# Scatters through disjoint views, later gathers, and copies kept in order in a routed expert layer

## The chip, the cores and the metric

The kernel runs on one core of a Trainium2 chip. The metric is the device time of one execution in microseconds (us); the median of three runs of the kernel before is 864.54 us (863.58 to 864.58). The profiled execution, from which all durations below are read, took 866.19 us, of which 864.5 us are its span from the first instruction to the last.

## The reference

Three layers on 3072 tokens of 512 numbers each, all float32:

```
attention: 4 batches x 8 heads x 768 positions x 64; a key is kept when it is one of the
           8 first or one of the 96 last; a bias by distance; softmax; a @ v
dense:     h = x @ w_in (512 x 2048); g = h if h > 0 else exp(h) - 1; y = g @ w_out
routed:    chosen = (y @ w_skip) > 0; expert = argmax(y @ w_gate) over 8; gate = its softmax weight
           out = y, and for chosen tokens  out = y + gate * (relu(y @ w1[expert]) @ w2[expert])
           (w1[e] 512 x 1024, w2[e] 1024 x 512)
```

## The kernel before

Every float32 product is made of three float16 products of high and low halves, so TensorE (PE) has much to do: 6233 matmuls. The tokens go through attention and the dense layer in 8 blocks (m = 0 to 7) of 3 tiles of 128 tokens; the attention of the next block is woven into the dense steps of the current one. A dense step (m, f), with f = 0 to 15, makes the product h (L439), a chain on ScalarE (ACT) and VectorE (DVE, L446) and GpSimd (POOL, L450) that ends in gs, and two steps later the product y from it (L460).

**Routing.** When a block's y is done, `route` copies it to yt (L504), writes it to the output (L506, or L589 for the last block), turns it with DMA transposes, takes the gate logits, and `place` computes for each token a slot in `xg`, a DRAM buffer of 8 experts x 256 rows of 514 numbers. `scatter(t)` (L582) is an indirect DMA on POOL's queue that writes the 128 rows of tile t into `xg`; a token that is not chosen gets a slot out of bounds and isn't written. Each row carries in its last column the token's number.

**Experts.** `ex_gather` (L635, SyncE's queue, SP) reads 128 rows of an expert back from `xg` to yg; `ex_tokens` (L644, L645) splits them into float16 halves eyh (one buffer for it) and turns them by DMA transpose (L646) to eyT. `ex_first` (L660, then L662 on ACT and L664 on DVE) and, two steps later, `ex_second` (L676) are the two products; the last step of an expert's tile adds the result to the row (eres, L684), copies the row's token number to integer (ix, L686) and scatters to the output (L687, POOL). `ex_prep` splits one piece of expert weights per tile and step (L623 on ACT, L624 on DVE) from er, loaded on SP (L608, L610) two pieces ahead into two stage buffers; a pair of loads waits for the split of the pair before.

`ex_tail` writes the order of this: steps s_ = 0 to 23 are experts 0 to 2 with their first tile of 128 slots, 24 to 47 the same experts with their second tile, then experts 3 to 6 with both tiles at once, then expert 7. The first tiles' gathers and splits stand earlier, in the dense steps f = 11 and f = 13 of the last block (L896). The last block itself is routed inside `ex_tail` (`ROUTE_LAST`: place at s_ = 11, its three scatters and its output writes at s_ = 12), the second tiles are gathered at s_ = 15, split at s_ = 22, 24 and 26, and the gathers of expert 3 stand at s_ = 38 and 39.

**What sets the order.** Each engine takes its instructions in a fixed order. A scheduler makes that order ahead of the run: it takes the instructions by the order in the program, but an instruction whose inputs are ready by its own reckoning passes others that are not. So an instruction can come ahead of its place in the program. `pin` (L72) ties an instruction behind the one written just before it on its engine. L623 and L644 are pinned, L686 is not. Waits between instructions come from a tracker of accesses to tiles and DRAM buffers: two indirect writes to `xg` may hit the same rows for all it knows, so the second waits until the first has landed, and a gather waits for all scatters before it.

Of the kernel before, what the change touches and what calls it, by code (L numbers as in the profile page):

```python
# [1 line left out]

# [10 lines left out]
U32 = DT.uint32  # L13
# [8 lines left out]
NT, DM, FF = 3072, 512, 2048  # L22
# [3 lines left out]
TB = 3  # L26
# [36 lines left out]
class Fast:  # L63
# [400 lines left out]
    def route_init(self):  # L464
        nc = self.nc
        self.wg = self.ct([P, ND, E + 1], F32, "wg")
        nc.sync.dma_start(self.wg[:, :, 0:E], self.a["moe2_w_gate"].rearrange("(c p) e -> p c e", p=P))
        nc.sync.dma_start(self.wg[:, :, E:E + 1], self.a["moe2_w_skip"].rearrange("(c p o) -> p c o", p=P, o=1))

        self.wgs = self.ct([P, ND, 2, E + 1], F16, "wgs")  # L470
        t = self.ct([P, ND, E + 1], F32, "wgt")
        nc.vector.tensor_scalar(t, self.wg, GS, None, ALU.mult)
        nc.vector.tensor_copy(self.wgs[:, :, 0, :], t)
        nc.vector.tensor_tensor(self.wgs[:, :, 1, :], t, self.wgs[:, :, 0, :], ALU.subtract)
        nc.vector.tensor_tensor(t, t, t, ALU.mult)
        self.wgm = self.ct([P, 2], F32, "wgm")
        nc.vector.tensor_reduce(out=self.wgm[:, 0:1], in_=t[:, :, 0:E], op=ALU.max, axis=AX.XY)
        nc.vector.tensor_reduce(out=self.wgm[:, 1:2], in_=t[:, :, E], op=ALU.max, axis=AX.X)
        self.esum = self.ct([P, TB], F32, "esum")
        nc.vector.memset(self.esum, 0.0)  # L480
        self.xg = self.dp.tile([E * CAP, ROW], F32, name="xg")
        z = self.zrow = self.mp.tile([P, ROW], F32, tag="yt", name="zrow", bufs=4)
        nc.gpsimd.memset(z[:, 0:DM + 1], 0.0)
        nc.gpsimd.memset(z[:, DM + 1:ROW], OOB)
# [5 lines left out]
    def route(self, m):  # L490

        nc, mp = self.nc, self.mp
        sm = mp.tile([P, 7, TB], F32, tag="sm", name=f"sm_{m}", bufs=2)
        oh = mp.tile([P, TB, E], F16, tag="oh", name=f"oh_{m}", bufs=2)
        pos = mp.tile([P, TB], I32, tag="pos", name=f"pos_{m}", bufs=2)
# [84 lines left out]

        def scatter(t):
            nc.gpsimd.indirect_dma_start(  # L582
                out=self.xg[:, :], out_offset=bass.IndirectOffsetOnAxis(ap=pos.bitcast(U32)[:, t:t + 1], axis=0),
                in_=yts[t][:, :], in_offset=None, bounds_check=E * CAP - 1, oob_is_err=False)

        def write():
# [4 lines left out]
        if last:  # L591
            return [evac, lambda: [turn(t) for t in range(TB)],
                    lambda: gate(0), lambda: gate(1), lambda: gate(2), place,
                    lambda: [scatter(t) for t in range(TB)], write]
        ops = dict(e=evac, a=lambda: turn(0), b=lambda: turn(1), c=lambda: turn(2), A=lambda: gate(0), B=lambda: gate(1),
                   C=lambda: gate(2), p=place, x=lambda: scatter(0), y=lambda: scatter(1), z=lambda: scatter(2))
        return [lambda w=w: [ops[o]() for o in w] for w in ROUTE]

# [69 lines left out]
    def ex_second(self, e, f, tiles):  # L668
        nc = self.nc
        hs = self.ehs.pop((e, f, tiles[0]))  # L670
        for j, t in enumerate(tiles):
            if f == 0:
                tag, bufs = ("pv", 1) if (e % 2 and t if e >= NX else e + t == 0) else ("acc", 3)
                self.eo[(e, t)] = self.ps.tile([P, DM], F32, tag=tag, name=f"eo_{e}_{t}", bufs=bufs)
            for n, (s_, x) in enumerate(((0, 0), (0, 1), (1, 0))):
                nc.tensor.matmul(self.eo[(e, t)], hs[:, s_, j * P:(j + 1) * P],  # L676
                                 self.ew[(e, 4 + f // 2, f % 2)][:, x, :],
                                 start=(f == 0 and n == 0), stop=(f == F2 // P - 1 and n == 2))
        if f < F2 // P - 1:
            return  # L680
        for t in tiles:
            y = self.eyg.pop((e, t))
            r = self.mp.tile([P, DM], F32, tag="yT", name=f"eres_{e}_{t}", bufs=2)
            nc.vector.scalar_tensor_tensor(r, self.eo.pop((e, t)), y[:, DM:DM + 1], y[:, 0:DM], ALU.mult, ALU.add)  # L684
            ix = self.xp.tile([P, 1], I32, tag="ix", name=f"ix_{e}_{t}", bufs=2 * E)
            nc.vector.tensor_copy(ix, y[:, DM + 1:DM + 2])  # L686
            nc.gpsimd.indirect_dma_start(  # L687
                out=self.out[:, :], out_offset=bass.IndirectOffsetOnAxis(ap=ix.bitcast(U32)[:, 0:1], axis=0),
                in_=r[:, :], in_offset=None, bounds_check=NT - 1, oob_is_err=False)

    def ex_tail(self, prep, rest):
        both = tuple(range(CAP // P))
        steps = [(e, f, (t,)) for t in both for e in range(NX) for f in range(F2 // P)]
        n0 = len(steps)
        steps += [(e, f, both) for e in range(NX, E - 1) for f in range(F2 // P)]
        steps += [(E - 1, f, (t,)) for t in both for f in range(F2 // P)]
        flag = self.flag()
        nf = F2 // P
        pieces = dict(zip("etABCpsw", self.route(NM - 1)))
        for s_, (e, f, tiles) in enumerate(steps):  # L700
            for x in ROUTE_LAST.get(s_, ""):
                pieces[x]()
            if s_ == 0:
                self.htags = "s0", "s1", "h"
            if s_ == 3:
                self.htags = ("h",)
            if s_ == 13:
                self.htags = "h", "s0", "h", "s1"
            if s_ == 15:
                for x in range(NX):  # L710
                    self.ex_gather(x, 1)
            for x in range(NX):
                if s_ == 22 + 2 * x:
                    self.ex_tokens(x, 1)
            if s_ == n0 - 10:
                self.ex_gather(NX, 0)
            if s_ == n0 - 9:
                self.ex_gather(NX, 1)
            if s_ in (n0 - 5, n0 - 3):
                self.ex_tokens(NX, (s_ - n0 + 5) // 2)  # L720
            if len(tiles) == 2 and e + 1 < E:
                if f == 1:
                    for t in both:
                        self.ex_gather(e + 1, t)
                if f in (3, 5):
                    self.ex_tokens(e + 1, (f - 3) // 2)
            self.ex_first(e, f, tiles)
            if s_ and rest:

                self.moe_y(*rest.pop(0))  # L730
            for _ in tiles:
                prep()
            if s_ >= 40:
                next(flag, None)
            if s_ == len(steps) - 1:
                for _ in flag:
                    pass
                self.flag_sum()
            if s_ >= XLAG:
                self.ex_second(*steps[s_ - XLAG])  # L740
        for x in steps[-XLAG:]:
            self.ex_second(*x)
        self.flag_all()
# [444 lines left out]
```

## Time and profile before

| | |
|---|---|
| median of the runs (lowest, highest) | 864.54 us (863.58, 864.58) |
| profiled execution: its own time, its span | 866.19 us, 864.5 us |
| PE busy | 817.8 us, 95% |
| DVE, ACT, POOL busy | 571.4, 530.0, 174.5 us |
| chain that ended last | PE 72%, DVE 11%, DMA 10% |
| mean granted TensorE clock | 0.977 |

A row of a timeline gives start, length, engine, line, operation, output <- inputs and how many instructions were merged; in brackets how long the engine had been idle before, and what ended that. PE shows as busy when it runs slowly too, so the granted clock belongs beside it. A DMA's row on SP or POOL is its issue alone; its landing is seen in the chain of waits or in the wait of whoever needs it.

### The profile page before, as it was taken

To read this page: it belongs to the slowest core of one execution; us is meant where nothing else is said; L and a number is where in the kernel's file an instruction comes from. 1 tells how busy PE (TensorE), PEld (TensorE's weight loads), DVE (VectorE), ACT (ScalarE), POOL (GpSimd) and SP (SyncE) were. 2 spreads that over 40 slices of the span, in tenths; PEclk is the share of its full clock that TensorE was granted. 3 is DMA by queue.
4 is the path that set the end of the run, shared out by engine and by line. 5 is a ranking of instruction groups with operands and counts; after the bars stand their busy time and mean duration, and the time that the engine had idled before them with its cause. 6 is when DMAs were issued, how large, how long until landed. Compare 5 with 4: busy or idle time off the path is not lost.

```text
span 864.5 us, 17637 instructions
## 1 busy us (share of the span) xinstructions
PE 817.8 (95%) x6233; PEld 479.4 (55%) x6233; DVE 571.4 (66%) x1951; ACT 530.0 (61%) x1310; POOL 174.5 (20%) x201
## 2 busy tenths in 40 slices
PE   6997989999999999999999999999998869999995
PEld 4773445555555555555555555555555637666663
DVE  6997997575467567556666765644666846878622
ACT  4775767777767677767776776645655425555311
POOL 1001112123222322321322232232231010101110
PEclk9997999999999999999999999999999988999998
DMA  7999973644686487688659656321646779779510
GB/s 293 256 298 253 245 217 91 132 111 102 201 205 162 137 214 142 175 191 189 152 139 229 154 124 146 77 51 43 189 154 159 228 225 211 247 242 275 157 44 26
DMA packets 185394, 148.80 MB, mean 172 GB/s; under 512 B 152208, under 2 KB 154256, under 8 KB 181200
## 3 DMA queue, kind: packets, MB, share of 16 engines
q1 hardware_dynamic: 182096, 141.59, 63.0%
q0 software_dynamic: 3200, 5.99, 1.9%
q8 instruction: 51, 0.84, 0.4%
q14 instruction: 47, 0.39, 0.2%
HBM read 94.82 MB, written 21.08 MB: 134 GB/s over the span
## 4 chain that ended last, share of the span: by engine, by line
PE 72%; DVE 11%; DMA 10%; issue 4%; POOL 1%; ACT 1%; SPq 0%; POOLq 0%; DVEq 0%; ACTq 0%
PE h L439 25%; PE y L460 24%; PE eh L660 7%; PE eo L676 6%; PE s L239 5%; PE pv L324 4%; DMA eyT<-eyh 3%; DMA xg<-yt,pos 2%; DMA yg<-xg 2%; DVE ew L624 2%; DVE wt L408 2%; DVE wt L409 1%; PE warm L354 1%; DMA xT<-xs 1%; DVE w L416 1%
## 5 line engine op out<-in xcount | busy, mean ns | idle before, releaser
L439 PE MATMUL h<-xT,w 128*128 128x384 f16 x1536 | 274.9, 329 | 4.1 <-DMA xT<-xs 4.1
L460 PE MATMUL y<-w,gs 128*128 128x512 f16 x1152 | 271.4, 381 | 0.0
L439 PEld LDWEIGHTS <-w 128*128 128x128 f16 x1536 | 146.8, 99 | 106.4 <-issue 9.7
L450 POOL TENSOR_TENSOR gs<-e,gs 128x384 f16<-128x384 f32 x128 | 126.1, 987 | 393.9 <-ACT gs L449 329.2
L460 PEld LDWEIGHTS <-gs 128*128 128x128 f16 x1152 | 110.8, 98 | 119.9 <-issue 2.7
L446 DVE SCALAR_TENSOR_TENSOR e<-e,h 128x384 f32<-128x384 f32 x128 | 70.4, 551 | 99.6 <-ACT e L444 94.1
L449 ACT ACTIVATE gs<-e 128x384 f16<-128x384 f32 x128 | 66.7, 522 | 86.1 <-DVE e L446 84.9
L253 ACT ACTIVATE p<-p,st 128x232 f32<-128x232 f32 (+1 forms) x192 | 89.2, 465 | 38.4 <-DVE st L248 37.7
L660 PE MATMUL eh<-eyT,ew 128*128 128x128 f16 (+1 forms) x1152 | 103.6, 243 | 7.6 <-DMA eyT<-eyh 5.6
L676 PE MATMUL eo<-ew,ehs 128*128 128x512 f16 x384 | 102.0, 388 | 8.1 <-DVE ehs L664 8.1
L660 PEld LDWEIGHTS <-ew 128*128 128x128 f16 x1152 | 88.7, 101 | 32.8 <-issue 6.7
L624 DVE SCALAR_TENSOR_TENSOR ew<-er,ew 128x512 f16<-128x512 f32 x128 | 90.5, 725 | 15.9 <-ACT ew L623 14.5
L443 ACT ACTIVATE e<-h 128x384 f32<-128x384 f32 x128 | 61.6, 481 | 58.5 <-PE h L439 54.5
L662 ACT ACTIVATE ehs<-eh 128x128 f16<-128x128 f32 (+1 forms) x96 | 29.9, 311 | 102.3 <-PE eh L660 99.8
L248 DVE CUSTOM_DVE_ANT_0 p<-s,tab 128x232 f32<-128x232 f32 (+1 forms) x192 | 67.1, 377 | 20.3 <-PE s L239 18.6
L623 ACT ACTIVATE ew<-er 128x512 f16<-128x512 f32 x128 | 75.4, 620 | 4.5 <-DMA er<-in_moe_w 4.2
L283 DVE TENSOR_TENSOR ph<-p,ph 128x464 f16<-128x464 f32 x68 | 43.1, 648 | 40.2 <-ACT ph L282 40.2
L444 ACT ACTIVATE e<-e 128x384 f32<-128x384 f32 x128 | 66.6, 520 | 2.5
L664 DVE SCALAR_TENSOR_TENSOR ehs<-eh,ehs 128x128 f16<-128x128 f32 (+1 forms) x96 | 31.9, 332 | 36.9 <-ACT ehs L662 36.7
L676 PEld LDWEIGHTS <-ehs 128*128 128x128 f16 x384 | 35.4, 99 | 36.7 <-DVE ehs L664 12.7
L687 POOL DMA_INDIRECT out<-eres,ix x16 | 16.9, 1053 | 161.9 <-DVE eres L684 117.7
L239 PE MATMUL s<-qh 64*128 64x232 f16 (+1 forms) x432 | 40.0, 254 | 3.1 <-DVE st L248 2.5
(171 smaller groups left out, 849.4 us busy)
## 6 DMA issues: line engine op xcount, KB each, us to landing
er<-in_moe_w SPq DMA_DIRECT2D x64, 512.0 KB
wr<-in_wf SPq DMA_DIRECT2D x16, 1024.0 KB
wc<-in_wf SPq DMA_DIRECT2D x16, 1024.0 KB
qk<-in_qk SPq DMA_DIRECT2D x20, 720.0 KB
out<-yt SPq DMA_DIRECT2D x24, 256.0 KB
rawv<-in_vp SPq DMA_DIRECT2D x21, 256.0 KB
xg<-zrow SPq DMA_DIRECT2D x16, 257.0 KB
yg<-xg SPq DMA_DIRECT2D x16, 257.0 KB
```

What stands on the lines that cost most here:

```text
L239: nc.tensor.matmul(sp[j], q[r, hp, KW:], k[r, hp, KW - w:KW], start=(x == 0), stop=(x == len(mm) - 1))
L248: nc.vector.tensor_tensor_reduce(pw[:, j, :], sp[j], self.tab[:, h, :] if i else self.tab0[:, h, :], -0.125, 3e38, ALU.add, ALU.min, st[:, ...
L253: nc.scalar.activation(pw[:, j, :], pw[:, j, :], AF.Exp, bias=st[:, 0, h:h + 1], scale=-1.0, accum_out=st[:, 1, h:h + 1])
L439: nc.tensor.matmul(hps, wi[:, s_, c, :], xT[:, x * ND + c, :], start=(n == 0), stop=(n == 3 * ND - 1))
L446: nc.vector.scalar_tensor_tensor(g, e, -HS, hps, ALU.mult, ALU.max, accum_out=self.gsum[:, m * NF + f:m * NF + f + 1])
L449: nc.scalar.activation(gs[:, 0], g, AF.Copy)
L450: nc.gpsimd.tensor_tensor(gs[:, 1], g, gs[:, 0], ALU.subtract)
L460: nc.tensor.matmul(self.ys[m][t], gs[:, s_, t * P:(t + 1) * P], wo[:, x, :], start=(f == 0 and n == 0), stop=(f == NF - 1 and n == 2))
L623: self.pin(nc.scalar.activation(w[:, 0], r, AF.Copy, scale=sc))
L624: nc.vector.scalar_tensor_tensor(w[:, 1], r, sc, w[:, 0], ALU.mult, ALU.subtract, accum_out=self.esums[:, c:c + 1])
L660: nc.tensor.matmul(hps, l, r, start=(i == 0), stop=(i == len(mm) - 1))
L676: nc.tensor.matmul(self.eo[(e, t)], hs[:, s_, j * P:(j + 1) * P], self.ew[(e, 4 + f // 2, f % 2)][:, x, :], start=(f == 0 and n == 0), sto ...
```

## The change

Three edits. The tracker is given three views of `xg` that it takes as disjoint, one for each tile of a block; `scatter(t)` of every block writes through view t. (Each token has a slot of its own.) Zeroing and gathers still use `xg` itself, which the tracker orders against all views. The gathers of the second tiles of experts 0 to 2 are written at s_ = 20 in place of s_ = 15. The 16 copies of token numbers at L686 are pinned, so each stands behind the eres of its tile.

```
+from concourse.bass_types import dram_disjoint_views
 ...
         self.xg = self.dp.tile([E * CAP, ROW], F32, name="xg")
+
+        self.xgs = dram_disjoint_views(self.xg[:, :], TB)
 ...
         def scatter(t):
             nc.gpsimd.indirect_dma_start(
-                out=self.xg[:, :], out_offset=bass.IndirectOffsetOnAxis(ap=pos.bitcast(U32)[:, t:t + 1], axis=0),
+                out=self.xgs[t][:, :], out_offset=bass.IndirectOffsetOnAxis(ap=pos.bitcast(U32)[:, t:t + 1], axis=0),
 ...
-            nc.vector.tensor_copy(ix, y[:, DM + 1:DM + 2])
+            self.pin(nc.vector.tensor_copy(ix, y[:, DM + 1:DM + 2]))
 ...
-            if s_ == 15:
+            if s_ == 20:
                 for x in range(NX):
                     self.ex_gather(x, 1)
```

## Rows read from the trace of the kernel before

**Rows 1.** Busy time by stretch: length, PE, PEld, DVE, ACT, POOL, clock, DMA, GB/s

```profile
450.00:600.00 150.00, 149.80 (x1127) 81.56 (x1126) 85.20 (x300) 96.46 (x234) 38.86 (x40) 1.00 0.50 116
...
700.00:714.00 14.00, 5.15 (x27) 1.85 (x26) 5.15 (x20) 1.08 (x3) 2.92 (x3) 0.66 0.84 229
...
733.00:748.00 15.00, 12.67 (x144) 8.78 (x143) 9.98 (x44) 7.85 (x20) 1.17 (x1) 1.00 0.81 262
```

**Rows 2.** Timeline of PE around the first expert products

```profile
637.92 2.11 PE L439 MATMUL h<-xT,w 128*128 128x384 f16 x12
...
645.71 2.11 PE L439 MATMUL h<-xT,w 128*128 128x384 f16 x12
...
655.44 2.11 PE L460 MATMUL y<-w,gs 128*128 128x512 f16 x9
660.11 2.68 PE L660 MATMUL eh<-eyT,ew 128*128 128x128 f16 x24 [2.56 <-DMA eyT<-eyh]
...
673.11 0.83 PE L660 MATMUL eh<-eyT,ew 128*128 128x128 f16 x12 [2.00 <-DVE ehs L664]
```

**Rows 3.** Timeline of DVE in the same stretch

```profile
641.28 0.56 DVE L446 SCALAR_TENSOR_TENSOR e<-e,h 128x384 f32<-128x384 f32 x1 [0.37 <-ACT e L444]
...
645.69 0.15 DVE L686 CAST ix<-yg 128x1 int32<-128x1 f32 x1 [3.85 <-DMA yg<-xg]
...
651.17 0.56 DVE L446 SCALAR_TENSOR_TENSOR e<-e,h 128x384 f32<-128x384 f32 x1
...
654.37 0.42 DVE L644 TENSOR_SCALAR eyh<-yg 128x512 f16<-128x512 f32 x1
```

**Rows 4.** Chain that ended last: start, us, what; first tiles

```profile
655.54 4.52 DMA eyT<-eyh
```

**Rows 5.** The same chain, the last block's scatters and the second tiles

```profile
689.11 6.46 DMA xg<-yt,pos
...
696.32 3.00 DMA xg<-yt,pos
...
700.07 2.83 DMA xg<-yt,pos
...
709.01 4.51 DMA eyT<-eyh
...
729.91 5.37 DMA yg<-xg
```

**Rows 6.** Timeline of SP: DMA issues between placing and gathering

```profile
689.07 4.62 SPq L608 DMA_DIRECT2D er<-in_moe_w  x3
702.91 1.38 SPq L635 DMA_DIRECT2D yg<-xg  x3
704.39 0.90 SPq L610 DMA_DIRECT2D er<-in_moe_w  x2
705.33 0.46 SPq L635 DMA_DIRECT2D yg<-xg  x1
```

**Rows 7.** Timeline of POOL: the last scatter and what follows

```profile
700.07 0.97 POOL L582 DMA_INDIRECT xg<-yt,pos  x1 [2.77 <-ACT ehs L662]
701.34 0.97 POOL L687 DMA_INDIRECT out<-eres,ix  x1 [0.30 <-issue]
```

**Rows 8.** Timeline of DVE around the second tiles

```profile
698.19 0.69 DVE L624 SCALAR_TENSOR_TENSOR ew<-er,ew 128x512 f16<-128x512 f32 x1
...
705.67 0.15 DVE L686 CAST ix<-yg 128x1 int32<-128x1 f32 x1 [6.78 <-DMA yg<-xg]
...
707.20 0.42 DVE L644 TENSOR_SCALAR eyh<-yg 128x512 f16<-128x512 f32 x1
...
725.29 0.43 DVE L644 TENSOR_SCALAR eyh<-yg 128x512 f16<-128x512 f32 x1 [0.94 <-DMA eyT<-eyh]
```

**Rows 9.** Timeline of PE around the second tiles

```profile
706.09 1.46 PE L676 MATMUL eo<-ew,ehs 128*128 128x512 f16 x3 [4.88 <-DVE ehs L664]
...
713.55 4.00 PE L660 MATMUL eh<-eyT,ew 128*128 128x128 f16 x36 [3.09 <-DMA eyT<-eyh]
```

## The prediction

> **What bounds the kernel now.** I read the busy times by stretch first. In the dense stage PE is busy 149.80 of 150 us at full clock; where PE is full, nothing that this change does on DVE, POOL or SP can shorten anything. Between 700 and 714 us it is different: PE is busy 5.15 of 14 us and the clock is at 0.66 of full; between 733 and 748 it is idle 15 - 12.67 = 2.33 us [rows 1]. So the time to be had lies in the tail, and the timelines of the engines there say who is late.
>
> The first gap is small: PE ends the product y that starts at 655.44 (2.11 long) at 657.55 and begins the first expert product at 660.11, idle 2.56 us, waiting for the transposed tokens eyT [rows 2]. DVE, which must split these tokens first, had stood still before: at 645.69 it runs a copy of token numbers (ix, L686) after 3.85 us in which it waited for a gather from xg [rows 3]. That copy is needed only eight steps later; it came ahead of its place because the scheduler reckoned the gather as landed. The reader should see a DVE that stands with work behind it, not a DVE that has none.
>
> The second gap is the large one. The last block's three scatters go one after another: the first takes 6.46 us to land, the second is issued at 696.32, the third at 700.07, landing at 702.90 [rows 5]. SP then issues the three gathers at 702.91 [rows 6]. Again ix copies stand in DVE's way: the one at 705.67 had held DVE for 6.78 us, and the split of the first second tile comes at 707.20 only [rows 8]. While DVE stands, PE lacks ehs for 4.88 us; then it lacks eyT for 3.09 us, and runs the expert step s_ = 24 at 713.55 [rows 9], at about half clock.
>
> **The change, part by part.**
>
> *Pinned copies, first gap.* Their wait goes. How late was DVE because of it? Before the stall, h that starts on PE at 637.92 is answered on DVE (L446) at 641.28, 3.36 us later. After it, h at 645.71 is answered at 651.17, 5.46 us later [rows 2, 3]. So 5.46 - 3.36 = 2.10 us of the stall were still there when the split eyh ran at 654.37, two weight splits behind it. Without the stall: eyh at 652.3, its transpose issued at 655.54 - 2.10 = 653.44, landed 4.52 later [rows 4] at 657.96, where y ends at 657.55. The wait left is 0.4 us. PE waits for DVE again at 673.11 (2.00 us) [rows 2], so from there on DVE's own shift counts: 2.1 us. Bounds: 0, if the ACT and weight splits before eyh set its time anyway; 3.7, if the slow clock that follows the gap goes too (the 24 products at 660.11 take 2.68 us where 12 take 0.83 at 673.11, so about 1 us, and as much in the y behind them, cut by what DVE allows). I take 2.1, the row's own lag.
>
> *Views, last block.* The second and third scatter no longer wait for a landing. POOL needs 1.27 us from one indirect DMA to the next when nothing holds it (700.07 to 701.34 [rows 7]), so issues at 689.11, 690.4 and 691.65. The landing of the third isn't shown by any row: the best case is 2.83 us (694.5), the worst 6.46 (698.1), as the first had it with output writes and weight loads in flight [rows 5]. Three weight loads fall in this stretch, issued from 689.07 to 693.69 [rows 6], so I go near the worst: 697.3. The Trainium skill (DMA: Bandwidth & Descriptors, section "Anatomy of one DMA — SWDGE (gpsimd) path") gives a software DMA about 2 us fixed plus bytes over 436 GB/s, most of the fixed part being the wait for the last write's receipt; for 257 KB that is an estimate of 2.6 us, near the 2.83 here and far from 6.46. By it the third would land at 694.3, and the sum below would gain 0.4 us more.
>
> Then the chain is followed with its own durations. Gathers at 697.35; the first landed within 2.7 us before (702.91 to the ix copy at 705.67 [rows 6, 8]), so 700.05. DVE's split can't come before about 699.7, since it stands behind the weight split of s_ = 21, the next but one after that of 698.19 [rows 8] (an estimate, 0.8 us behind its end). With no ix ahead it runs at 700.1. From split to issue of the transpose it took 1.17 us at 654.37 [rows 3, 4], so with the product halves between it about 1.2: 701.3, in place of 709.01 [rows 5]. That is 7.7 us. All that follows (4.51 us of transpose, the next split, the next transpose) is the same chain moved. PE's step 24 comes at 705.9 where it came at 713.55. Bounds: 8.1, from the floor of 699.7; 4.3, if the gather takes 5.37 us as a later one did [rows 5] and the scatter lands at 698.1.
>
> *Views, blocks 0 to 6.* Their scatters wait for each other as well, but PE is full there [rows 1]: 0. Were gs on POOL late there, it would show as PE idle; 0.2 us in 150 bounds it.
>
> *Gathers at s_ = 20.* On SP they are moved past the loads of s_ = 16 and 18. In the trace these loads already run before the gathers (the three from 689.07 [rows 6]), so by itself this costs and earns 0. It matters for what the views do: gathers that are ready earlier could now pass these two loads, and the later place works against that. If they pass, see the second rival.
>
> *Pinned copies, the rest.* 16 copies of 0.15 us [rows 8] move behind their eres. Nothing waits on DVE for a pinned one, as eres must be done before it anyway. All but the last lie beside PE work; the last stands between the last eres and the last output scatter: 0.1 us lost, at most 0.15. The gaps between 733 and 748 us hang on gathers that wait for a buffer to come free (729.91 [rows 5]) and on a split pinned elsewhere; no edit touches them: 0, with ends of -2.3 and +2.3.
>
> **Sum.** 2.1 + 7.7 - 0.1 = 9.7 us. Against the profiled execution: 866.19 - 9.7 = 856.5. That execution lies 1.65 above the median of the runs, so for the median 864.54 - 9.7 = 854.8 us.
>
> **Rivals.**
>
> *Gathers pass the loads (gain 6).* If SP's order puts the gathers before the loads of s_ = 16 and 18, SP stands there until the scatters land, and these loads go out some 5 us late. ACT then waits for weights, and DVE's split of s_ = 21, behind which the tokens' split is pinned, moves to about 703.3, 3.5 us behind the forecast: 858.3. For it: gathers ready 3 to 5 us earlier, and a scheduler that lets ready work pass. Against: at s_ = 20 the loads stand first in the program.
>
> *Scatters still one behind another (gain 4).* Then the gathers stay at 702.91, and only the copies' waits go: split at 705.67 in place of 707.20, with 0.4 to 0.6 us of further waits behind it, some 2.1 us. 2.1 + 2.1 - 0.1: 860.4. Against: at 701.34 POOL issues an output scatter while the scatter of 700.07 is still in flight until 702.90 [rows 5, 7], so the queue itself takes a second. The Trainium skill (DMA: Bandwidth & Descriptors, section "SWDGE vs HWDGE vs iDMA") says that only one software queue is allocated, which speaks for this case; no row here shows two scatters to xg in flight.
>
> *All gaps shrink (gain 13).* If the clock stays up through both gaps and the waits of 733 to 748 go, about 1.5 and 2 us more: 851.5. Against: nothing in the edits touches the latter.
>
> *Slower.* There is one buffer for split tokens (eyh), and expert 3's first tile wants it too: its split was run at 725.29 [rows 8], far ahead of its place at s_ = 43. With all gathers ready sooner, the scheduler may put it before the second tile of expert 0. Its gather is the fourth (issued at 705.33, 2.4 us behind the first [rows 6]). Then DVE stands till about 703 to 706, its transpose of 4.51 goes first, and expert 0's split comes near 711.5, its transpose lands at 717.2, PE's step 24 is 3.7 us later than now. 3.7 - 2.1 + 0.1 = 1.7 slower: 866.2. It decides from the point where the scheduler reckons the fourth gather as landed before the weight split of s_ = 21. Against: before, it came last of the four.
>
> **Chances.** Forecast 0.57 (852.5 to 857), gathers pass 0.18, scatters in line 0.09, all gaps 0.08, slower 0.05, and 0.03 that a change in the order eats the gain to nothing. About 0.2% (1.7 us) is what a measurement here can tell from no change. Faster 0.91, same 0.04, slower 0.05. The range goes from 850 (3.7 + 8.1 + 2.3 is 14.1, so 850.4) to 860.8, which takes in the scatters in line.
>
> **What would show it.** In the changed trace: no ix copy on DVE with a wait for a gather; the three scatters within 3 us on POOL; the gathers on SP at 696 to 698 on the old clock (694 to 696 with the first gap's gain) and behind the loads; PE's step 24 some 10 us earlier, idle before it about 3 us in place of 8; eyh for expert 0 ahead of expert 3's. Wrong if the step 24 doesn't move, if PE between 450 and 600 is less than full, or if the idle time comes back at 715 to 748.

## The result, and the profile after

The changed kernel is slower: 874.37 us median of 9 runs (869.63 to 877.12) against 866.58 us of 9 runs of the kernel before (863.58 to 868.10), a ratio of 1.0099 [1.0079, 1.0118]. The forecast was 854.8 us, and the range ended at 860.8. The profiled execution took 873.99 us (span 872.3), 7.80 us more than the one of before. Lines of the changed kernel are one to three higher (L663 is L660 of before, L689 is L686); experiments that keep the old file keep the old numbers.

I read it stage by stage, by the stretches of TensorE (PE). Changed kernel, busy time by stretch; columns as in [rows 1]:

```profile
300.00:450.00 150.00, 149.22 (x1148) 80.57 (x1148) 94.48 (x327) 106.55 (x268) 37.36 (x38) 1.00 0.69 172
450.00:600.00 150.00, 149.59 (x1125) 81.19 (x1125) 84.87 (x303) 96.06 (x236) 37.09 (x39) 1.00 0.52 117
...
750.00:850.00 100.00, 89.93 (x630) 59.19 (x628) 53.05 (x195) 34.21 (x77) 7.77 (x8) 0.93 0.54 153
```

The same stretch of the kernel before:

```profile
750.00:850.00 100.00, 100.00 (x774) 68.50 (x772) 64.10 (x235) 40.81 (x93) 10.61 (x10) 1.00 0.57 172
```

The reader should see the last row of the first fence: where PE had been full at full clock, it now stands 10.07 us and runs at 0.93. The prediction had not looked at this stretch at all. The timeline of PE says where it stands (changed kernel):

```profile
659.35 1.51 PE L663 MATMUL eh<-eyT,ew 128*128 128x128 f16 x24 [0.32 <-DMA eyT<-eyh]
671.73 0.83 PE L663 MATMUL eh<-eyT,ew 128*128 128x128 f16 x12 [2.99 <-DVE ehs L667]
...
707.02 3.92 PE L663 MATMUL eh<-eyT,ew 128*128 128x128 f16 x36 [4.97 <-DMA eyT<-eyh]
...
787.34 2.74 PE L663 MATMUL eh<-eyT,ew 128*128 128x256 f16 x12 [6.16 <-DMA eyT<-eyh]
814.85 2.72 PE L663 MATMUL eh<-eyT,ew 128*128 128x256 f16 x12 [3.91 <-DMA eyT<-eyh]
```

The first three rows answer to [rows 2] and [rows 9]: step 24 comes at 707.02 where it came at 713.55, so up to there the change gains 6.53 us. The last two are new: the first products of experts 5 and 6 wait for their transposed tokens, 6.16 and 3.91 us, and run at half clock behind the wait (2.74 us where the same 12 products take 1.47 later on). The granted clock, the last number but two, is 0.50 there:

```profile
787.40:792.30 4.90, 4.90 (x18) 2.57 (x19) 1.68 (x7) 1.42 (x3) 0.00 (x0) 0.50 0.67 261
```

**Where these two waits come from.** SP's issues around expert 5, changed kernel:

```profile
767.62 0.38 SPq L613 DMA_DIRECT2D er<-in_moe_w  x1
768.05 0.95 SPq L638 DMA_DIRECT2D yg<-xg  x2
769.04 5.17 SPq L613 DMA_DIRECT2D er<-in_moe_w  x2
774.48 1.23 SPq L649 DMA_TRANSPOSE eyT<-eyh  x1
...
782.77 1.23 SPq L649 DMA_TRANSPOSE eyT<-eyh  x1
```

and in the kernel before:

```profile
774.20 0.33 SPq L635 DMA_DIRECT2D yg<-xg  x1
775.42 0.38 SPq L610 DMA_DIRECT2D er<-in_moe_w  x1
776.08 0.33 SPq L635 DMA_DIRECT2D yg<-xg  x1
...
778.77 1.23 SPq L646 DMA_TRANSPOSE eyT<-eyh  x1
...
784.19 1.23 SPq L646 DMA_TRANSPOSE eyT<-eyh  x1
```

And DVE of the changed kernel in the same stretch:

```profile
765.63 0.74 DVE L687 SCALAR_TENSOR_TENSOR eres<-eo,yg 128x512 f32<-128x512 f32 x1
766.30 0.68 DVE L627 SCALAR_TENSOR_TENSOR ew<-er,ew 128x512 f16<-128x512 f32 x1
...
767.52 0.15 DVE L689 CAST ix<-yg 128x1 int32<-128x1 f32 x1
767.58 0.74 DVE L687 SCALAR_TENSOR_TENSOR eres<-eo,yg 128x512 f32<-128x512 f32 x1
...
768.24 0.14 DVE L689 CAST ix<-yg 128x1 int32<-128x1 f32 x1
...
772.76 0.43 DVE L647 TENSOR_SCALAR eyh<-yg 128x512 f16<-128x512 f32 x1 [1.63 <-DMA yg<-xg]
...
781.11 0.43 DVE L647 TENSOR_SCALAR eyh<-yg 128x512 f16<-128x512 f32 x1 [4.03 <-issue]
```

Four buffers hold the gathered rows yg, so expert 5's gathers need those of expert 3's tiles. Before, the last reader of such a buffer was eres: the copy ix, not pinned, ran soon after the gather's landing. Pinned, ix is the last reader, and two weight splits stand between it and its eres (766.30 to 767.52). The buffer comes free later, and SP's order is another: a weight load, both gathers together, two more loads. Put on one clock (the changed kernel is about 8.3 us ahead here), the delay grows along the chain: the first gather is 768.05 - (774.20 - 8.3) = 2.15 us late, the first transpose 774.48 - 770.47 = 4.0, the last one 782.77 - 775.89 = 6.9. The step from 4.0 to 6.9 has a cause of its own: eyh has one buffer, so the second split waits until the first transpose has landed. That took 6.6 us here (774.48 to 781.11); before, it took 4.2 at most, as the split of 783.00 didn't wait behind the transpose of 778.77. For expert 6, where it is the same, the profile names what the split waited for:

```profile
810.09 0.43 DVE L647 TENSOR_SCALAR eyh<-yg 128x512 f16<-128x512 f32 x1 [3.99 <-DMA eyT<-eyh]
```

Before, the last transpose of expert 5 was issued 5.2 us ahead of its use (784.19; the product starts at 789.38). With a transpose of 4.5 us that was 0.7 us of slack; 6.9 - 0.7 is 6.2 us, the wait that PE shows.

The ledger, each at the same instruction: 2.05 us gained at the first scatter (687.06, was 689.11), 4.5 more at step 24, 1.8 more up to step 48 (all three 8.4), then 16.2 lost: 744.71 to 872.3 is 127.6 us, where 753.08 to 864.5 was 111.4. Of these, 10.1 are the two waits and 5.4 the slow products behind them (PE is busy 107.40 us in this part, where it was busy 101.98): 15.5. The other 0.6 lies behind the last output scatter: from its issue to the end it is 8.9 us, 8.3 in the kernel before, and 7.8 to 8.9 in the other runs, so it isn't put down to the edits. 8.4 - 16.2 = -7.8, as measured.

### The profile page after: what moved, and what is told of

The parts are those of the page before. It is cut to its first block, busy times and chain, and to the rows that moved or that the text cites. A ratio compares the mean times of both kernels' runs of the same rounds, so it can differ in the third digit from the quotient of the medians.

```text
span 872.3 us, 17639 instructions
## 1 busy us (share of the span) xinstructions
PE 817.1 (94%) x6233; PEld 478.5 (55%) x6233; DVE 568.4 (65%) x1951; ACT 529.4 (61%) x1310; POOL 171.9 (20%) x201
## 4 chain that ended last, share of the span: by engine, by line
PE 68%; DVE 12%; DMA 10%; issue 5%; POOL 2%; ACT 2%; SPq 0%; DVEq 0%; POOLq 0%; ACTq 0%
PE h L440 22%; PE y L461 21%; PE eh L663 6%; PE eo L679 6%; PE s L240 5%; PE pv L325 4%; DMA eyT<-eyh 4%; DVE ew L627 2%; PE warm L355 2%; DVE wt L409 1%; DVE wt L410 1%; DVE e L447 1%; DMA xg<-yt,pos 1%; DMA er<-in_moe_w 1%; DMA xT<-xs 1%
## 5 line engine op out<-in xcount | busy, mean ns | idle before, releaser
L451 POOL TENSOR_TENSOR gs<-e,gs 128x384 f16<-128x384 f32 x128 | 123.0, 964 | 429.6 <-ACT gs L450 369.7
L663 PE MATMUL eh<-eyT,ew 128*128 128x128 f16 (+1 forms) x1152 | 104.4, 243 | 18.4 <-DMA eyT<-eyh 15.4
L663 PEld LDWEIGHTS <-ew 128*128 128x128 f16 x1152 | 88.1, 100 | 45.4 <-issue 13.8
```

The costliest lines, as they stand in the source:

```text
L451: nc.gpsimd.tensor_tensor(gs[:, 1], g, gs[:, 0], ALU.subtract)
L663: nc.tensor.matmul(hps, l, r, start=(i == 0), stop=(i == len(mm) - 1))
```

## The experiments

Theory A: the late copy holds the gather's buffer, and this alone makes the loss. Rival B: the gain itself does it, as the tail comes 8 us earlier and meets the weight loads another way. Theory C: not the buffer but the copy's place on DVE. Theory D: the views cost time in the dense stage.

**e1: the pins alone** (kernel before, plus)

```
-            nc.vector.tensor_copy(ix, y[:, DM + 1:DM + 2])
+            self.pin(nc.vector.tensor_copy(ix, y[:, DM + 1:DM + 2]))
```

> The kernel before with the 16 copies of token numbers pinned and nothing else. Theory A (buffer held): behind a pinned copy, two weight splits later than eres, the yg buffer of experts 3 and 4 comes free later, the gathers of experts 5 and 6 go out later and behind a weight load, and PE waits for eyT at both; that part of the trace cost 16 us in the changed kernel. A expects both waits here, 16 us, less some 4 us from copies that no longer hold DVE: ratio to before about 1.014. Theory B (earlier work meets the weight loads): the waits at experts 5 and 6 come from the 8 us that the work before them gained, which puts transposes among other loads. B expects no such waits here and a ratio of 0.995 to 1.000.

872.79 us against 865.84, ratio 1.0081 [1.0049, 1.0113]. PE's timeline and SP's, in this order:

```profile
787.01 2.74 PE L660 MATMUL eh<-eyT,ew 128*128 128x256 f16 x12 [4.09 <-DMA eyT<-eyh]
813.91 2.72 PE L660 MATMUL eh<-eyT,ew 128*128 128x256 f16 x12 [3.30 <-DMA eyT<-eyh]
```

```profile
769.21 0.94 SPq L635 DMA_DIRECT2D yg<-xg  x2
770.20 5.10 SPq L610 DMA_DIRECT2D er<-in_moe_w  x2
```

Without views and later gathers both waits are there, with the two gathers together and loads behind them, and the kernel is slower. The waits are smaller (7.4 us of idle in place of 10.1), and the loss is smaller than A's 1.014. This kernel also shows what the pins alone earn ahead of them: step 24 at 709.64, 3.9 us earlier than before.

**e2: views and s_ = 20, no pins** (changed kernel, but)

```
-            self.pin(nc.vector.tensor_copy(ix, y[:, DM + 1:DM + 2]))
+            nc.vector.tensor_copy(ix, y[:, DM + 1:DM + 2])
```

> The views and the gathers at s_ = 20, the copies not pinned. Theory A: no wait for eyT at experts 5 and 6, the part from step 50 on is 111.4 us as in the kernel before; the gap before step 24 shrinks by 4 to 7 us: ratio 0.992 to 0.996. Theory B: step 24 comes earlier, so the waits at experts 5 and 6 are there, several us each: ratio over 1.003.

863.91 us, ratio 0.9976 [0.9959, 0.9993]; PE busy 100.00 of 100 us from 750 to 850, no wait at experts 5 and 6. Step 24 at 709.03, 4.5 us earlier, of which 3.3 are left at the last output scatter, so the tail is shifted here too. The gain is less than I expected: the ix copies still stand in DVE's way (at 701.02 one has held it for 3.48 us).

**e3: all three edits, pins for experts 0 to 2 only**

```
-            self.pin(nc.vector.tensor_copy(ix, y[:, DM + 1:DM + 2]))
+            (self.pin if e < NX else id)(nc.vector.tensor_copy(ix, y[:, DM + 1:DM + 2]))
```

> All three edits, but copies pinned only for experts 0 to 2. Theory A: all of the gain before step 48 (8.3 us in the changed kernel's trace) and no wait for eyT at experts 5 and 6: ratio about 0.990. Theory B: the same shift, so the same waits: ratio about 1.009, like the changed kernel.

860.85 us, ratio 0.9962 [0.9916, 1.0009], which by itself doesn't exclude no change; one of its five runs took 868.77. The trace is clear: PE is busy 99.56 of 100 us from 750 to 850 and no wait for eyT is left. The loss goes with the pins of experts 3 to 7, which did nothing for the two gaps.

**e4: the copies pinned right behind the split** (e2, and the copy moved from L686 into `ex_tokens`)

```
 (behind the transpose of L646)
+        ix = self.ix[(e, t)] = self.xp.tile([P, 1], I32, tag="ix", ...)
+        self.pin(nc.vector.tensor_copy(ix, self.eyg[(e, t)][:, DM + 1:DM + 2]))
 (in place of L685, L686)
+            ix = self.ix.pop((e, t))
```

> Views and gathers at s_ = 20; each copy is made right behind the split of its row (L645) and pinned there, so it neither waits for a gather by itself nor holds a buffer after eres. Theory A: ratio about 0.990, no wait for eyT at experts 5 and 6. Theory B: ratio about 1.009 with both waits.

859.87 us, ratio 0.9936 [0.9915, 0.9957]. No wait at experts 5 and 6; step 24 at 708.23. The copy stands in program order and still leaves the buffer to eres: this kernel is faster than the kernel before and than the changed one, though its gain is short of the 0.990 expected. B falls with e2 to e4: none has the waits, and at expert 3's eres, whose buffer is the one at stake, they are 3.3, 5.5 and 6.3 us earlier than the kernel before. e1, which has the waits, is 6.6 earlier there; e9 below is 8.4 earlier, more than the changed kernel's 7.8, and has none.

**e5: all three edits, but the pinned copy reads a side tile**

```
 (behind the transpose of L649)
+        k = self.tk[(e, t)] = self.xp.tile([P, 1], F32, tag="tk", ..., bufs=8)
+        self.pin(nc.vector.tensor_copy(k, self.eyg[(e, t)][:, DM + 1:DM + 2]))
-            ix = ... bufs=2 * E)
-            self.pin(nc.vector.tensor_copy(ix, y[:, DM + 1:DM + 2]))
+            ix = ... bufs=E)
+            self.pin(nc.vector.tensor_copy(ix, self.tk.pop((e, t))))
```

> All three edits, but each pinned copy reads the token numbers from a small tile of its own, filled right behind the split of the row, so it stands where it stood on DVE and no longer holds the yg buffer. If the held buffer is what costs (theory A), the waits for eyT at experts 5 and 6 are gone and the ratio to before is 0.992 to 0.996, as with the copy made at the split. If it is the place of 16 pinned copies on DVE itself (theory C), the waits stay and the ratio is 1.005 to 1.009.

861.45 us against 865.11, ratio 0.9946 [0.9919, 0.9974]. (The tile ix has 8 buffers here in place of 16; nothing in the trace waits for one.) DVE's timeline, and then SP's:

```profile
769.17 0.75 DVE L684 SCALAR_TENSOR_TENSOR eres<-eo,yg 128x512 f32<-128x512 f32 x1
...
771.06 0.15 DVE L686 CAST ix<-tk 128x1 int32<-128x1 f32 x1
```

```profile
769.95 0.33 SPq L635 DMA_DIRECT2D yg<-xg  x1
771.17 0.38 SPq L610 DMA_DIRECT2D er<-in_moe_w  x1
771.89 0.33 SPq L635 DMA_DIRECT2D yg<-xg  x1
```

The pinned copy stands as late as in the changed kernel, 1.1 us behind its eres, and there are as many of them. But it reads tk, the gather goes out 0.03 us after eres ends, ahead of the copy, and PE is busy 100.00 of 100 us. So C falls, and A holds: it is the read of yg that costs, not the place.

**e6: the views alone** (e2, and the line below); **e8: views and pins** (changed kernel, and the same line)

```
-            if s_ == 20:
+            if s_ == 15:
```

> The views alone: gathers at s_ = 15, copies not pinned. If the later gathers are what keeps the gathers behind the weight loads (the second rival of the prediction), one load goes out late here and step 24 is 2 to 4 us later than with views and s_ = 20 (709.03 in that trace); if not, the two agree within 1 us. Dense stage: theory D, that scatters issued in a row on POOL hold gs back, expects PE between 150 and 600 some 1 us less busy than before (449.1 of 450); without it 449.0 to 449.2 is only noise and the kernel before, run again, would show it too. Ratio 0.997 to 1.000.

> The changed kernel with its gathers back at s_ = 15. If the later place is worth nothing, as I costed it, the ratio is that of the changed kernel, 1.008 to 1.010. If it kept the gathers behind the weight loads, this one is 2 to 4 us slower still: 1.011 to 1.014.

e6: 863.67 us, 0.9981 [0.9952, 1.0010]. SP's timeline shows what s_ = 20 is for:

```profile
697.82 1.27 SPq L635 DMA_DIRECT2D yg<-xg  x3
699.15 0.42 SPq L608 DMA_DIRECT2D er<-in_moe_w  x1
```

At s_ = 15 the gathers pass one weight load, and step 24 comes at 711.11, 2.1 us later than in e2 (0.6 of it e6 was late already at the first scatter). The times of e6 and e2 can't be told apart all the same. e8: 872.23 us, 1.0068 [1.0038, 1.0098], with both waits (4.54 and 2.81 us); that is below either of the two ratios expected, and its interval overlaps that of the changed kernel. What s_ = 20 is worth in the end stays open.

**e7: views for the last block only** (e4, and)

```
-                out=self.xgs[t][:, :], ...
+                out=(self.xgs[t] if last else self.xg)[:, :], ...
```

> Copy made at the split, gathers at s_ = 20, and the views for the last block's scatters alone; the earlier blocks' scatters wait for each other as before. Theory D expects the dense stage back at before's pace, 1 to 2 us faster than with views everywhere: ratio 0.991 to 0.993 against 0.9936 with views everywhere. If the views cost nothing there, the ratio stays at 0.9936.

861.11 us, ratio 0.9938 [0.9912, 0.9964], as e4. Busy time by stretch:

```profile
300.00:450.00 150.00, 149.80 (x1157) 81.11 (x1155) 96.68 (x328) 106.94 (x268) 37.61 (x38) 1.00 0.71 172
450.00:600.00 150.00, 149.80 (x1140) 81.60 (x1135) 85.95 (x305) 96.86 (x238) 38.25 (x40) 1.00 0.51 117
```

PE is full again, as before and in e1. The changed kernel, e2 to e6 and e8, all with views in every block, show less (149.12 to 149.59 from 450 to 600). Over the whole stretch that e6's expectation named, 150 to 600, PE is busy 449.08 us in the kernel before, 449.07 in e1 and 448.89 in e7, but 448.13 in e6 and 447.69 to 448.56 in the others with views in every block. So D is shown in the rows; at the same instructions it costs 1.3 to 2.3 us (worked out under "Views in blocks 0 to 6" below). In the time it isn't shown: e7 is no faster than e4. Its first expert product starts at 660.54, 0.45 us later than e4's, but its profiled execution was already 2.6 us behind the kernel before at the first h of block 2, where e4's was 0.1 ahead; from there to the last block it loses nothing. What makes executions differ so early isn't known.

**e9 and e10: the last block's output writes left out, and moved.** Why does the third scatter land 7.19 us after its issue in the changed kernel (7.20 in e4)?

```
-ROUTE_LAST = {3: 'et', 7: 'A', 8: 'B', 9: 'C', 11: 'p', 12: 'sw'}
+ROUTE_LAST = {3: 'et', 7: 'A', 8: 'B', 9: 'C', 11: 'p', 12: 's'}            (e4 to e9)
+ROUTE_LAST = {3: 'et', 5: 'w', 7: 'A', 8: 'B', 9: 'C', 11: 'p', 12: 's'}    (e4 to e10)
```

> The copy-at-the-split kernel (views, gathers at s_ = 20, token numbers copied and pinned right behind the split) without the last block's three output writes of 256 KB (left out: these 384 rows keep only the expert results). It asks why the last block's third scatter lands 7.2 us after its issue (690.90 to the gathers at 698.12) and not 5.65 as forecast. Theory L, the DMA engines are full: between 690 and 697 us they move 339 GB/s at a share of 1.02, three output writes (0.79 MB) and three weight loads (1.57 MB) beside the scatters; 2.36 MB at 0.33 MB per us is 7 us. Without the writes the gathers stand 4.5 to 5.5 us behind the third scatter's issue, and step 24 on PE comes 1.5 to 2.5 us earlier, near 706. Rival Q, the queue: three scatters in one queue land one after another with 2.8 us each whatever else moves; then the distance stays within 0.5 us of 7.2.

> The copy-at-the-split kernel with the last block's output writes at s_ = 5 in place of s_ = 12, ahead of the gates and the placing, where nothing waits for a DMA of this size. By theory L the third scatter lands 4.5 to 5.5 us after its issue as without the writes, step 24 comes near 706 to 707, and the time is 1.5 to 2 us below the copy-at-the-split kernel's: a ratio of 0.990 to 0.993 to the kernel before, where that one had 0.9936. By rival Q nothing moves: 0.9936. Slower than 0.9936 if the writes at s_ = 5 hold SP's queue, or the transposes of the last block's tokens, so that the gates come late and the scatters with them.

The chain of waits of e9, then of e10:

```profile
690.31 6.61 DMA xg<-yt,pos
```

```profile
693.46 6.00 DMA xg<-yt,pos
```

Both expectations of theory L failed: without the writes the stretch from 690 to 697 moves 216 GB/s at a DMA share of 0.64 in place of 339 at 1.02, and the landing is only 0.6 us shorter, 1.2 in e10; step 24 comes at 707.30 and 709.99. By the letter Q failed too, as it allowed 0.5. What Q says of the queue can be seen from other scatters of the changed kernel. Below are the times from issue to landing of three that are issued in a row: first those of the last block, then those issued at 570.06, 571.36 and 572.63.

```profile
DMA to landing us min/median/max: 6.2/6.3/7.2
```

```profile
DMA to landing us min/median/max: 2.4/2.6/2.6
```

The second three stand as close behind one another as the first, and still each lands 2.4 to 2.6 us after its own issue. So they don't land one after another, and Q falls. What differs most is the traffic beside them: the share of the DMA engines is 0.15 from 570 to 575.2 and 0.93 from 687 to 697. (They also move less, 0.27 MB against at most 0.66, so the traffic isn't tried by itself.) A single scatter with nothing else in its queue took 6.46 us in such traffic (a share of 0.99 from 689 to 695.6) in the kernel before [rows 5]. The output writes are the smaller part of it, by e9 and e10; weight loads are issued beside the scatters in both, and how much of the 6.0 to 6.6 us that are left is theirs wasn't tried. e10 takes 859.90 us against 865.37, 0.9930 [0.9910, 0.9949], not to be told from e4. Its first scatter is issued at 690.91, 2.6 us later than in e4 (688.34), but its profiled execution was 1.8 us behind e4's in the dense stage already, ahead of all that was moved; what the earlier writes are worth stays open. e9 has a single run (858.40 us).

## Why the prediction was wrong

**The step that failed** is "Pinned copies, the rest", costed at 0.1 us with the reason "Nothing waits on DVE for a pinned one, as eres must be done before it anyway". That looked at who waits for the copy's result. The copy also reads yg, and who waits for that is SP's next gather, which needs the buffer. As the last reader the copy held it past eres; 0.1 us was in truth two waits of 10.1 us and their slow clock, 15.5 in all. e1 has the loss with the pins alone, e3 to e5 take away the buffer's late release and it is gone. The rival "slower" looked for its mechanism in eyh's one buffer, at the second tiles; the mechanism was of that kind, but it started with yg's four buffers, and eyh's one only made the delay longer. I had even named a gap that hangs on gathers waiting for a buffer [rows 5], and said that no edit touches it.

**First gap, 2.1 forecast:** the mechanism was right. No ix copy holds DVE there, and PE's wait is 0.32 us (forecast 0.4). The size was too small, and that the first scatter comes 2.05 us earlier is chance: a larger gain less a loss that was not forecast. The h that started at 645.71 [rows 2] is 1.48 us late in the changed kernel:

```profile
647.19 2.11 PE L440 MATMUL h<-xT,w 128*128 128x384 f16 x12
```

From there to the first scatter 1.48 + 2.05 = 3.5 us are gained. 2.24 of them are the wait; most of the others are the slow clock behind it, which is gone too (granted clock 1.00 from 659.4 to 663, was 0.50 from 660.2 to 663; the 24 products take 1.51 us for 2.68). The forecast had this as its upper bound of 3.7 and took the lower value. e1, with the pins alone, gains 3.3 in the same stretch, e3 to e5 1.9 to 2.7. Of the 1.48 us lost ahead of it 1.3 belong to the views, below.

**Second gap, 7.7 forecast:** the mechanism was right, the size 4.5. The scatters went out at 687.06, 688.35 and 689.62, 1.28 apart as forecast, and SP issued the gathers behind the loads. The chain of waits of the changed kernel:

```profile
689.62 7.19 DMA xg<-yt,pos
...
696.83 2.69 DMA yg<-xg
...
699.55 0.43 DVE eyh L647
...
700.81 6.17 DMA eyT<-eyh
```

Two terms were mis-sized. The third landing took 7.19 us for 5.65, beyond even the 6.46 that I called the worst; the first two took 6.2 and 6.3, so in this traffic the worst case was the usual one. The transpose took 6.17 for 4.51 [rows 5]; two weight loads and a gather were sent between 698.23 and 699.17, just ahead of it, but whether they are the reason wasn't tried. 1.54 + 1.66 = 3.2 is the difference. The gather's 2.69 (forecast 2.7) and split to issue, 1.26 (1.2), were right. The Trainium skill (DMA: Bandwidth & Descriptors, "Anatomy of one DMA — SWDGE (gpsimd) path"), whose 2 us plus bytes gave an estimate of 2.6, is near the three in a row of 570 us (2.4 to 2.6, with 0.27 MB in all) and far from those beside loads and writes (6.2 to 7.2).

**Views in blocks 0 to 6, costed at nothing, bounded by 0.2 in 150:** too low, and a sign that the prediction named itself, PE between 450 and 600 less than full, is there (149.59 us for 149.80). The scatters no longer wait, so the scheduler sets all three ahead of gs on POOL (changed kernel):

```profile
418.62 1.19 POOL L585 DMA_INDIRECT xg<-yt,pos  x1 [4.92 <-DVE pos L579]
420.12 1.52 POOL L585 DMA_INDIRECT xg<-yt,pos  x1 [0.30 <-issue]
421.94 0.97 POOL L585 DMA_INDIRECT xg<-yt,pos  x1 [0.30 <-issue]
422.93 1.80 POOL L451 TENSOR_TENSOR gs<-e,gs 128x384 f16<-128x384 f32 x2
```

Before, a gs stood between the first and the second:

```profile
418.04 1.19 POOL L582 DMA_INDIRECT xg<-yt,pos  x1 [4.92 <-DVE pos L576]
419.48 1.50 POOL L450 TENSOR_TENSOR gs<-e,gs 128x384 f16<-128x384 f32 x1 [0.25 <-ACT gs L449]
```

In the profile's groups PE's idle time ahead of y, none before, is now:

```profile
L461 PE MATMUL y<-w,gs 128*128 128x512 f16 x1152 | 271.0, 380 | 0.5 <-POOL gs L451 0.5
```

What it costs is read at the same instructions. The first h of block 2 (226.20 before) comes 0.17 us late in the changed kernel, the h of 645.71 1.48 late: 1.3 us lost between them. The other kernels with views in every block lose 1.3 to 2.3 us in the same stretch, e1 and e7, without them, nothing (0.03 and -0.04). A wait that goes also lets its instruction pass others.

**Waits from 715 to 748, costed at nothing (ends -2.3 and +2.3):** 1.8 us gained between steps 24 and 48, within the ends; which edit gave them wasn't tried apart.

**Gathers at s_ = 20:** on SP as said: e2 has them behind the loads, e6 ahead of one. "Gathers pass the loads" (rival, costed at 3.5 us, though its own 703.3 is 3.2 behind 700.1) was real for s_ = 15, at 2.1 us on step 24.

Had the failed step cost the 0.1, some 873.99 - 15.5 = 858.5 us would have been left for the profiled execution: a gain of 7.7 for the forecast 9.7. The kernels that do without the held buffer gain less: the ratios of e3 to e5 (0.9936 to 0.9962) are 3.3 to 5.5 us of 864.54. So 9.7 was too much even without the failed step: the second gap gave 3.2 less and the views took 1.3. Why the changed kernel is ahead of these three up to expert 3 (7.8 us, where they have 5.5, 6.3 and 4.3) isn't shown.

## What to carry to other kernels

Before an instruction is moved later, list what it reads as well as who reads it: as the last reader of a buffer it decides when the next transfer into that buffer can start. If a value is wanted late, copy it out early (e4, e5), and put the copy where its input is already known to be there. And look at the slack of the stretches that are full, too: here a transpose that had 0.7 us to spare turned a delay of 2 us into waits of 10. Last, don't take an agreement of two totals for an agreement of terms: 2.05 us for 2.1 was a gain of 3.5 less a loss of 1.5, and a run with one edit alone (e1) helps to tell them apart.

## What the runs showed of the hardware

Three indirect scatters can be in flight on POOL's queue, 1.28 us apart in issue, and each lands by itself: 2.4 to 2.6 us after its issue where the share of the DMA engines was 0.15 (570 to 575.2 us, changed kernel), 6.2 to 7.2 where it was 0.93 (687 to 697). The longest landing of a scatter in that kernel is 9.4 us, at a share of 1.00 (269.3 to 280).

A transpose of a split tile took 3.05 us where SP had sent no load for 6 us and the share of the DMA engines was 0.46 (811.76, changed kernel), and 4.5 to 6.7 us at three other places of the same chain with shares of 0.98 to 1.11 (782.77, 700.81, 803.32). What makes the difference among these three wasn't tried.
